# Fresh buffers for the butterflies, later exchange sums, and a down end in five banks, in a fused spectral filter and gated MLP

## The chip, the cores and the metric

The kernel runs on one core of a Trainium2 chip. The metric is the device time of one execution in microseconds (us), the median of several runs. A profile of one execution is read beside it.

## The reference

A layer norm feeds two branches, and their sum is added to the input. One branch is a two-dimensional real FFT over the sequence (2048) and the features (448), a product with a complex filter, and the inverse FFT. The other is a gated MLP with a hidden width of 1792.

```python
def _A_ref(x, w_r, w_i):
    X = jnp.fft.rfft2(x, axes=(-2, -1)) * (w_r + 1j * w_i)
    return jnp.fft.irfft2(X, (S, D), axes=(-2, -1))

def _B_ref(x, W_gate, W_up, W_down):
    gate, up = x @ W_gate, x @ W_up
    return ((gate * (gate > 0)) * up) @ W_down

x = A_x                                   # (1, 2048, 448), f32
xn = _layernorm(x, axis=-1)
return x + _A_ref(xn, A_w_r, A_w_i) + _B_ref(xn, B_W_gate, B_W_up, B_W_down)
```

## The kernel before

**Number format.** Every f32 operand of a matmul is split into a high and a low f16 part, and three matmuls (high by high, high by low, low by high) stand for one. ACT writes the high part, VectorE the low part (value less high part).

**Rows.** The 2048 rows lie as 16 tiles of 128 (`n2` = 0 to 15), in four chunks (`q = n2 % 4`, in the order 0, 2, 1, 3). A tile is normalised (`ln_xn` on VectorE, `ln_hi` on ACT, `ln_lo` on VectorE), and its f16 parts are transposed into `Tq[q]`: in the opening by TensorE or by DMA, in chunks 1 and 3 by DMA (`ln_dma`). `ln_norm` does the first steps for chunks 1 and 3.

**The foreground: the MLP.** The hidden width is 14 blocks of 128 (`f`), in three groups of 5, 5 and 4. A gate unit `("gu", g, f, q)` computes gate and up of one block for one chunk into a PSUM tile of two banks (`gu`, two of them), with 20 full matmuls (L721) and a few of half height (L728). Then `gu_post` runs: relu on ACT (L758), the product with up on VectorE (L762, the last reader of the banks), the high part on ACT (L766) and the low part on VectorE (L770). A down unit `("dn", g, n2)` multiplies all blocks of a group into one PSUM bank (`dn`, two of them; L789), and `dn_post` (L795) adds that to the output tile `xy[:, n2]` on VectorE. After the last gate unit come the four down units of chunk 3: tiles 3, 7, 11 and 15. `store` sends a tile out when both branches have been added.

**The background: the FFT.** It stands in a list `bg` of small steps, each with a cost in us of VectorE. Per tile: a DFT over the features on TensorE (`f_dft`), sums on VectorE (`f_eo`, `f_x`), a split, a DFT over 128 rows (`f_sdft`). Across the 16 tiles: four stages of butterflies on VectorE (`bfly`, called by `f_y1`, `stage2`, `stage3`, `stage4`), on f32 tiles of 128 x 456 in a pool of 17 buffers (`ybuf`, handed out from the list `free`, the last freed first). Then the exchange: `swap` copies the rows 1 to 63 and 65 to 127 crosswise into one of four buffers `sw` by two DMAs on SP's queue (L517, L518), and `pair` adds them (L523, L524). `wmul` multiplies by the filter (L490 to L493). The inverse does the same backwards: butterflies, `i_swap`, `i_pair`, `i_mix` (L590 to L596), splits (L604, L610), `i_sdft` (L620), splits (L625, L628), `i_ddft` (L639) and `i_acc` (L644), which adds to `xy`. `i_sdft` and `i_ddft` use two PSUM banks (`fx`). The list `il` says how many blocks apart the steps of one inverse tile stand.

**The order.** The opening is written out by hand. After that the program walks the units. With each unit it takes background steps from `bg` as long as the unit's credit lasts: a share of the unit's time (`took`) less its own VectorE work (`fixed`). The share is one number, found by bisection so that the background is used up at the unit `last_gu`. Weight preparation is placed by `sched` so many gate units ahead of its use: the down weights' squares, scale, high and low halves (`wd_sq`, `wd_sum`, `wd_scale`, `wd_hi`, `wd_lo`) 4, 3 and 2 units ahead. Within these bounds a list scheduler orders the instructions of each engine; every engine works its own queue in order. All DMAs of this kernel are issued by SP.

Of the kernel before, what the change touches and what calls it, by code (L numbers as in the profile page):

```python
# [42 lines left out]
EXPONE = float(1 << 23)  # L43
NSW = 4
SQ = 2.0 ** -16

# [98 lines left out]
def tile_gfnet_reglu(ctx: ExitStack, tc: tile.TileContext, x, xr, wgu, wd, wf, ident, c_fd, c_fm, c_im, c_row, c_id,  # L145
# [116 lines left out]
    def ln_rstd(q, js=(0, 1, 2, 3), bias=False):  # L262
        w, m = rst[q, js[0]]
        sd, r0, t, r, nm = (w[:, i] for i in range(5))
        V.reciprocal(r0, sd)
        V.scalar_tensor_tensor(t, m[:, :, 1], 1e-5, r0, op0=OP.add, op1=OP.mult)
        V.scalar_tensor_tensor(t, t, -0.5 * 2048, r0, op0=OP.mult, op1=OP.mult)
        V.scalar_tensor_tensor(r, t, 1.5 * 2048, r0, op0=OP.add, op1=OP.mult)
        if bias:
            V.scalar_tensor_tensor(nm, m[:, :, 0], -1.0, r, op0=OP.mult, op1=OP.mult)  # L270
        for i, j in enumerate(js):
            rst[q, j] = r[:, i:i + 1], nm[:, i:i + 1], m[:, i, 0:1]
# [30 lines left out]
    def ln_norm(n2):  # L303
        ln_xn(n2)
        ln_hi(n2)
        ln_copy(n2)
        free.append(xr_b.pop(n2))

    def ln_lo(n2):
        x, t = xn[n2], tt[n2].rearrange("p a b -> p (a b)")  # L310
        V.tensor_tensor(t[:, 512:896], x[:, 0:384], t[:, 0:384], op=OP.subtract)
        twice = [v[:, None, :].to_broadcast([128, 2, 64]) for v in (x[:, 384:448], t[:, 384:448])]
        V.tensor_tensor(tt[n2][:, 3:9:5, 64:128], *twice, op=OP.subtract)
        G.tensor_copy(tt[n2][:, 8, 0:48].rearrange("p (a b) -> p a b", b=16), tt[n2][:, 4:7, 112:128])
        free.append(xn_b.pop(n2))
# [72 lines left out]
    def bfly(a, b, p, sgn):  # L388

        if p == 0:  # L390
            t = free.pop()
            V.tensor_tensor(t, a, b, op=OP.add)  # L392
            V.tensor_tensor(b, a, b, op=OP.subtract)  # L393
            free.append(a)
            return t, b
        t = free.pop()
        if p == 4:
# [17 lines left out]
        V.scalar_tensor_tensor(b, t, f, a, op0=OP.mult, op1=OP.add)  # L415
        V.scalar_tensor_tensor(a, t, -f, a, op0=OP.mult, op1=OP.add)
        free.append(t)
        return b, a

    def f_y1(n2):  # L420
        if n2 < 8:
            t = free.pop()
            A.activation(t, yps[n2], AF.Copy)
            cur["y", n2] = t
        else:
            a, ps = cur.pop(("y", n2 - 8)), yps[n2]
            t = free.pop()
            V.tensor_tensor(t, a, ps, op=OP.add)
            V.tensor_tensor(a, a, ps, op=OP.subtract)
            cur["s1", n2 - 8, 0], cur["s1", n2 - 8, 1] = t, a  # L430

# [53 lines left out]

    def wmul(k2):
        xt, w = cur.pop(("X", k2)), wf_t[k2]
        t = free.pop()
        bc = [w[:, i, :, None, :].to_broadcast([128, 4, 2, KC]) for i in range(2)]
        V.tensor_tensor(t, xt, bc[0], op=OP.mult)  # L490
        V.tensor_tensor(xt, xt, bc[1], op=OP.mult)  # L491
        V.tensor_tensor(t[:, :, 0], t[:, :, 0], xt[:, :, 1], op=OP.subtract)
        V.tensor_tensor(t[:, :, 1], t[:, :, 1], xt[:, :, 0], op=OP.add)  # L493
        free.append(xt)
        cur["V", k2] = t

# [89 lines left out]
    def i_mix(n2):  # L586

        u = cur.pop(("U", n2))
        t = free.pop()
        V.tensor_tensor(t[:, 0:2], u[:, 0:2], u[:, 2:4], op=OP.add)  # L590
        V.tensor_tensor(u[:, 0:2], u[:, 0:2], u[:, 2:4], op=OP.subtract)
        V.tensor_tensor(t[:, 2], t[:, 0], t[:, 1], op=OP.add)
        V.tensor_tensor(t[:, 3], t[:, 0], t[:, 1], op=OP.subtract)
        t2, u2 = (b.rearrange("p g c k -> p (g c) k") for b in (t, u))
        V.tensor_tensor(t2[:, 0:4:3], u2[:, 0:2], u2[:, 3:1:-1], op=OP.subtract)
        V.tensor_tensor(t2[:, 2:0:-1], u2[:, 0:2], u2[:, 3:1:-1], op=OP.add)  # L596
        free.append(u)
        cur["Q", n2] = t
# [194 lines left out]

    def dn_post(g, n2):
        last["V"] = V.scalar_tensor_tensor(xy[:, n2, :], dps[n2][:, 0:D], dsc[:, g:g + 1], xy[:, n2, :],  # L795
                                           op0=OP.mult, op1=OP.add).ins

    def store(n2):

        if n2 in stored:  # L800
            nc.sync.dma_start(ov[:, n2, :], xy[:, n2, :])
        stored.add(n2)

# [9 lines left out]
    def ln_chunk(q):  # L813
        for j in range(4):
            add(0.79, ln_stats, q, j)
        add(0.0, ln_sd, q)
        add(0.7, ln_rstd, q)
        n = [q + 4 * j for j in (0, 2, 1, 3)]
        for t in range(4 + 2):
            for st, (c, fn) in reversed(list(enumerate(((0.51, ln_norm), (0.78, ln_lo), (0.0, ln_dma))))):  # L820
# [5 lines left out]
    fl = ((0.0, f_dft), (0.77, f_eo), (1.08, f_x), (0.63, f_lo), (0.0, f_sdft), (None, f_y1))  # L826
    bf = (1.26, 2.04, 2.04, 2.04, 1.56, 2.04, 2.04, 2.04)

    def fft_chunk(q):
        n = [q + 4 * j for j in (0, 2, 1, 3)]  # L830
        for t in range(4 + len(fl) - 1):
            for st in reversed(range(len(fl))):
                i = t - st
                if 0 <= i < 4:
                    add(fl[st][0] if st < 5 else 1.25 * (n[i] >= 8), fl[st][1], n[i])

# [31 lines left out]
    def back(k0):  # L868
        add(bf[0], inv1, k0)
        if k0 >= 4:  # L870
# [7 lines left out]
            lambda: row_dft(1), row_ev]  # L878
    rows_us = [0.0, 0.8, 0.0, 1.2, 0.0, 0.4, 0.0, 0.8]


    for i0 in range(10):
# [6 lines left out]
        for k in pair_k:  # L889
            add(0.78, pair, ("X", k), 1)  # L890
        if i0 < 8:
            for k in (k0, k0 + 8):
                add(0.0, swap, ("X", k))
        for k in (ks[i0 - 1], ks[i0 - 1] + 8) if 0 < i0 < 9 else ():
            add(0.0, wneg, k)
        for k in pair_k:
            add(2.04, wmul, k)
            add(0.0, wsq, k)
# [4 lines left out]
    add(0.1, wsq_fin)  # L903
    add(0.8, wsq_scale)
    for c, fn in zip(rows_us[4:], rows[4:]):
        add(c, fn)

    def i_wait(n2):
        pass

    il = ((0.0, i_swap), (0.0, i_wait), (0.78, i_pair), (1.86, i_mix), (0.0, i_hi), (0.69, i_lo), (0.0, i_sdft),
          (0.0, i_pqhi), (0.69, i_pqlo), (0.0, i_ddft), (0.68, i_acc))
    io = [n for n0 in range(8) for n in (n0, n0 + 8)]
    for t in range(16 + len(il) - 1):
        if t < 16 and t % 2 == 0:
            add(bf[t // 2], stage4, t // 2, -1, "i3", "U")
        if 3 <= t < 19:
            add(0.0, load_im, io[t - 3])
        for st in reversed(range(len(il))):
# [74 lines left out]
    for g, fs in enumerate(groups):  # L994
        s = max(i for i in gus if i < first["dn", g])
        if g:
            for i, f in enumerate(fs):
                sched(gslot(s, 4), wd_sq, i, f)
            sched(gslot(s, 4), wd_sum, len(fs))
            sched(gslot(s, 3), wd_scale, g, fs)  # L1000
            for i, f in enumerate(fs):
                sched(gslot(s, 2 - i // 2), wd_hi, i, f)
                sched(gslot(s, 2 - i // 2), wd_lo, i, f)
            for i, f in enumerate(fs):
# [75 lines left out]
    took = lambda u: 4.55 if u[0] == "gu" else 0.56 * len(groups[u[1]])  # L1080
    V_US = {"w_scale": 0.33, "w_lo": 0.75, "wd_scale": 1.5, "wd_lo": 0.68}

    def fixed(i):
        c = 1.37 if units[i][0] == "gu" else 0.68
        return c + sum(V_US.get(fn.__name__, 0.0) for fn, a in at.get(i, []))

# [3 lines left out]

    last_gu = max(gus) - 6
    lo, hi = 0.3, 1.2
# [13 lines left out]
    for i, u in list(enumerate(units))[len(groups[0]):]:  # L1106
        is_gu = u[0] == "gu"
        if is_gu:
            _, g, f, q = u
            run_bg(until=marks["T", q])  # L1110
            gu_unit(f, q, (mates.get(u) or (0, 0, None, None))[2:])
        else:
            _, g, n2, _ = u
            dn_mm(groups[g], n2)
        with after(LAG):
# [6 lines left out]
            run_bg(amount=room(i, load[0]) if i >= RAMP else 0.0)  # L1122
        if is_gu:
            with tc.high_priority(offset=400):
# [7 lines left out]
        act_anchors.append(last["A"])  # L1132
    run_bg(until=len(bg))


# [43 lines left out]
```

## Time and profile before

| | before |
|---|---|
| median of three runs | 452.87 us (452.42 to 453.21) |
| profiled execution | 452.37 us, span 450.6 us |
| TensorE (PE) busy | 438.8 us, 97% |
| VectorE (DVE) busy | 390.3 us, 87% |
| ScalarE (ACT) busy | 182.3 us, 40% |
| GpSimd (POOL) busy | 28.1 us, 6% |
| granted TensorE clock | 1.000 |

Busy time is the union of an engine's instructions. Rows of a group read: line, engine, operation, written tile and read tiles, shapes, count, then busy us and mean ns of one, then idle time before them and who ended it. Rows in order of time read: start, length, engine, line, operation, shapes, count of merged instructions, and in brackets the idle time before them and its releaser.

### The profile page before, as it was taken

What the parts mean: (1) busy time and instruction counts of PE and PEld (TensorE: products, weight loads), DVE (VectorE), ACT (ScalarE), POOL (GpSimd) and SP (SyncE); (2) the same over time, 40 slices, a digit from 0 to 9 for tenths busy, and PEclk for the clock granted to TensorE, in tenths of its full rate; (3) what the DMA queues carried; (4) which work ended last, traced back from release to release, by engine and by line L of the source; (5) the groups of instructions that cost most, each with busy time, mean ns of one, the idle gap of its engine ahead of it and who ended that gap; (6) DMA issues with size and microseconds to landing.
All of it is one profiled execution on the core that took longest, in us unless ns stands there. A gap on an engine that the chain in (4) does not pass through costs nothing.

```text
span 450.6 us, 7312 instructions
## 1 busy us (share of the span) xinstructions
PE 438.8 (97%) x2613; PEld 218.2 (48%) x2613; DVE 390.3 (87%) x963; ACT 182.3 (40%) x390; POOL 28.1 (6%) x89
## 2 busy tenths in 40 slices
PE   7999999999999999999999999999999999999996
PEld 3544645455455444444444444444444545655652
DVE  6988799989779888999999999998999997987442
ACT  5887233543545573143134344333234234134120
POOL 2320030200000120000000000000000000000000
PEclk9999999999999999999999999999999999999999
DMA  7939963220002452250320210001111210200202
GB/s 257 328 84 280 397 226 79 49 57 2 1 1 69 154 161 80 84 149 25 90 69 8 83 35 0 1 1 63 62 54 48 90 42 25 88 33 33 89 35 81
DMA packets 39084, 39.61 MB, mean 88 GB/s; under 512 B 18454, under 2 KB 34952, under 8 KB 39048
## 3 DMA queue, kind: packets, MB, share of 16 engines
q1 hardware_dynamic: 39048, 39.15, 27.4%
q8 instruction: 20, 0.33, 0.3%
q14 instruction: 16, 0.13, 0.1%
HBM read 24.38 MB, written 3.67 MB: 62 GB/s over the span
## 4 chain that ended last, share of the span: by engine, by line
PE 48%; DVE 40%; DMA 5%; issue 3%; ACT 2%; SPq 1%; POOL 0%; DVEq 0%; ACTq 0%
PE gu L721 24%; PE dn L789 14%; DVE g L762 4%; DVE h L770 3%; DMA sw<-y 3%; DVE xy L795 2%; PE fx L356 2%; DVE y L490 2%; DVE wt L675 2%; PE fx L386 2%; DVE y L393 2%; PE fx L639 2%; DVE y L392 2%; DVE y L491 2%; PE fx L620 2%
## 5 line engine op out<-in xcount | busy, mean ns | idle before, releaser
L721 PE MATMUL gu<-T,wt 128*128 128x512 f16 (+1 forms) x1140 | 255.9, 375 | 1.6 <-DVE g L762 1.4
L721 PEld LDWEIGHTS <-wt 128*128 128x128 f16 x1140 | 108.8, 98 | 130.1 <-issue 9.7
L789 PE MATMUL dn<-wdt,h 128*128 128x448 f16 x672 | 135.9, 352 | 1.1 <-DVE xy L795 0.9
L789 PEld LDWEIGHTS <-h 128*128 128x128 f16 x672 | 65.1, 98 | 62.8 <-issue 2.6
L766 ACT ACTIVATE h<-g 128x512 f16<-128x512 f32 x56 | 35.0, 626 | 70.7 <-DVE g L762 70.5
L758 ACT ACTIVATE g<-gu 128x512 f32<-128x512 f32 x56 | 33.0, 589 | 72.4 <-PE gu L728 51.5
L770 DVE TENSOR_TENSOR h<-g,h 128x512 f16<-128x512 f32 x56 | 38.3, 686 | 7.2 <-ACT h L766 7.0
L762 DVE SCALAR_TENSOR_TENSOR g<-gu,g 128x512 f32<-128x512 f32 x56 | 38.4, 685 | 6.1 <-ACT g L758 6.0
L795 DVE SCALAR_TENSOR_TENSOR xy<-dn,dsc,xy 128x448 f32<-128x448 f32 x48 | 32.4, 679 | 10.0 <-PE dn L789 10.0
L604 ACT ACTIVATE vt<-y,fsc 128x456 f16<-128x456 f32 x16 | 10.7, 674 | 40.5 <-PE fx L620 26.3
L671 ACT ACTIVATE wt<-wst,wsc 128x512 f16<-128x512 f32 x28 | 19.1, 713 | 5.6 <-DVE wsc L195 5.5
L644 DVE SCALAR_TENSOR_TENSOR xy<-fx,fsc,xy 128x448 f32<-128x448 f32 x16 | 10.8, 681 | 11.6 <-PE fx L639 11.6
L675 DVE SCALAR_TENSOR_TENSOR wt<-wst,wsc,wt 128x512 f16<-128x512 f32 x28 | 20.4, 746 | 0.0
L185 ACT ACTIVATE junk<-wst 128x512 bf16<-128x512 f32 x28 | 17.4, 622 | 2.2 <-DMA wst<-in_wgu 1.9
L728 PE MATMUL gu<-T,wt 64*128 64x512 f16 x112 | 17.0, 381 | 1.1 <-DVE g L762 1.0
L188 POOL PARTITION_ALL_REDUCE wm<-wm x15 | 6.6, 443 | 164.0 <-ACT junk L185 164.0
L523 DVE TENSOR_TENSOR y<-y,sw 128x228 f32<-128x228 f32 x32 | 12.4, 389 | 4.1 <-DMA sw<-y 4.1
L393 DVE TENSOR_TENSOR y<-y,y 128x456 f32<-128x456 f32 x22 | 13.9, 631 | 2.2 <-DMA row<-y 1.7
L377 ACT ACTIVATE Xh<-X 128x456 f16<-128x456 f32 x16 | 9.2, 578 | 14.4 <-PE fx L386 8.1
L625 ACT ACTIVATE pgh<-fx 114x512 f16<-114x512 f32 x16 | 9.5, 592 | 13.1 <-PE fx L639 12.9
L620 PEld LDWEIGHTS <-vt 128*128 128x128 f16 x192 | 12.1, 98 | 4.2 <-issue 0.4
L392 DVE TENSOR_TENSOR y<-y,y 128x456 f32<-128x456 f32 x22 | 13.8, 628 | 0.3
(120 smaller groups left out, 456.7 us busy)
## 6 DMA issues: line engine op xcount, KB each, us to landing
sw<-y SPq DMA_DIRECT2D x64, 112.2 KB
wst<-in_wgu SPq DMA_DIRECT2D x28, 256.0 KB
wf<-in_wf SPq DMA_DIRECT2D x16, 228.0 KB
y<-in_xr SPq DMA_DIRECT2D x16, 224.0 KB
xy<-in_x SPq DMA_DIRECT2D x16, 224.0 KB
out<-xy SPq DMA_DIRECT2D x16, 224.0 KB
wdst<-in_wd SPq DMA_DIRECT2D x14, 224.0 KB
fm<-in_c_fm SPq DMA_DIRECT2D x4, 256.0 KB
```

The lines of the kernel that those rows point to most:

```text
L392: V.tensor_tensor(t, a, b, op=OP.add)
L393: V.tensor_tensor(b, a, b, op=OP.subtract)
L620: P.matmul(o, v[:, h, w], m[:, c, :], start=(i == 0), stop=(i == 2), skip_group_check=True)
L671: A.activation(w[:, 0:4, :], wst[f, g], AF.Copy, scale=wsc[f, g])
L675: V.scalar_tensor_tensor(w[:, 4:8, :], st, sc, w[:, 0:4, :], op0=OP.mult, op1=OP.subtract)
L721: last["P"] = P.matmul(hps[f, q][:, g, cs], wt[f, g][:, a, :], Tq[q][:, b, cs], start=(start and i == 0), stop=(stop and i == len(seq) - 1 ...
L758: last["A"] = A.activation(g1s[f, q], hps[f, q][:, 0, :], AF.Relu, scale=2.0 ** -22).ins
L762: last["V"] = V.scalar_tensor_tensor(g1, hps[f, q][:, 1, :], 2.0 ** -22, g1, op0=OP.mult, op1=OP.mult).ins
L766: A.activation(ht[f, q][:, 0, :], g1s[f, q], AF.Copy)
L770: V.tensor_tensor(h[:, 1, :], g1s.pop((f, q)), h[:, 0, :], op=OP.subtract)
L789: last["P"] = P.matmul(ps[:, 0:D], ht[f, q][:, a, js], wdt[f][:, b, :], start=(i == 0), stop=(i == n - 1)).ins
L795: last["V"] = V.scalar_tensor_tensor(xy[:, n2, :], dps[n2][:, 0:D], dsc[:, g:g + 1], xy[:, n2, :], op0=OP.mult, op1=OP.add).ins
```

## The change

1. A butterfly writes both results into buffers that it takes from the pool, instead of one over an input; `f_y1` and `i_mix` likewise. The pool has 18 buffers, and the one freed longest ago is handed out first.
2. `wmul` does both tiles of a pair with their steps interleaved; `i_mix` has another order of its six operations.
3. In the inverse, `i_pair` and what follows it stand one block later behind `i_swap`.
4. In chunks 1 and 3 ACT subtracts the mean and scales the f16 copy; VectorE's `tensor_scalar` is gone, and the low half multiplies by the row's factor itself.
5. The cost table of the background is new, `last_gu` lies one place later, and the down weights are prepared two gate units earlier.
6. The last four down units become one step, `dn_end`: block by block instead of tile by tile, in five PSUM banks (two `dn`, one half of each `gu` tile, one `fx`), the last tile in two halves of its columns; the additions come behind the last block.

```diff
+LASTGU = 5
-    ybuf = [mt([128, 4, 2, KC], F32, f"y{i}") for i in range(17)]
+    ybuf = [mt([128, 4, 2, KC], F32, f"y{i}") for i in range(18)]
...
+        elif q in CHUNKS[2:]:
+            V.tensor_scalar(nm, m[:, :, 0], -1.0, None, op0=OP.mult)
...
     def ln_norm(n2):
-        ln_xn(n2)
-        ln_hi(n2)
+        xn_b[n2] = free.pop(0)
+        xn[n2] = xn_b[n2].rearrange("p g c k -> p (g c k)")[:, 0:D]
+        r, nm, _ = rst[n2 % 4, n2 // 4]
+        A.activation(xn[n2], xr_t[n2], AF.Identity, bias=nm)
+        new_tt(n2)
+        A.activation(tt[n2].rearrange("p a b -> p (a b)")[:, 0:D], xn[n2], AF.Copy, scale=r)
...
     def ln_lo(n2):
+        if n2 % 4 in CHUNKS[2:]:
+            r = rst[n2 % 4, n2 // 4][0]
+            V.scalar_tensor_tensor(t[:, 512:896], x[:, 0:384], r, t[:, 0:384], op0=OP.mult, op1=OP.subtract)
+            V.scalar_tensor_tensor(tt[n2][:, 3:9:5, 64:128], x2, r, t2, op0=OP.mult, op1=OP.subtract)
...
     def bfly(a, b, p, sgn):
         if p == 0:
-            t = free.pop()
+            t, d = free.pop(0), free.pop(0)
             V.tensor_tensor(t, a, b, op=OP.add)
-            V.tensor_tensor(b, a, b, op=OP.subtract)
-            free.append(a)
-            return t, b
+            V.tensor_tensor(d, a, b, op=OP.subtract)
+            free.extend((a, b))
+            return t, d
...
+        d = free.pop(0)
         V.scalar_tensor_tensor(b, t, f, a, op0=OP.mult, op1=OP.add)
-        V.scalar_tensor_tensor(a, t, -f, a, op0=OP.mult, op1=OP.add)
-        free.append(t)
-        return b, a
+        V.scalar_tensor_tensor(d, t, -f, a, op0=OP.mult, op1=OP.add)
+        free.extend((a, t))
+        return b, d
...
-    def wmul(k2):
+    def wmul(*ks2):
+        ts = []
+        for k2 in ks2:
...
+            V.tensor_tensor(t, xt, bc[0], op=OP.mult)
+            ts.append((t, xt, bc[1]))
+        for t, xt, w in ts:
+            V.tensor_tensor(xt, xt, w, op=OP.mult)
+        for k2, (t, xt, w) in zip(ks2, ts):
+            V.tensor_tensor(t[:, :, 0], t[:, :, 0], xt[:, :, 1], op=OP.subtract)
+            V.tensor_tensor(t[:, :, 1], t[:, :, 1], xt[:, :, 0], op=OP.add)
...
     def i_mix(n2):
+        t, s = free.pop(0), free.pop(0)
+        V.tensor_tensor(s[:, 0:2], u[:, 0:2], u[:, 2:4], op=OP.subtract)
+        V.tensor_tensor(s[:, 2:4], u[:, 0:2], u[:, 2:4], op=OP.add)
+        V.tensor_tensor(t2[:, 0:4:3], s2[:, 0:2], s2[:, 3:1:-1], op=OP.subtract)
+        V.tensor_tensor(t2[:, 2:0:-1], s2[:, 0:2], s2[:, 3:1:-1], op=OP.add)
+        V.tensor_tensor(t[:, 2], s[:, 2], s[:, 3], op=OP.add)
+        V.tensor_tensor(t[:, 3], s[:, 2], s[:, 3], op=OP.subtract)
...
+    def dn_end(g, ns):
+        fs = groups[g]
+        banks = [psum.tile([128, 512], F32, name="dn", bufs=2) for _ in range(2)]
+        banks += [psum.tile([128, 2, 512], F32, name="gu", bufs=2)[:, 0] for _ in range(2)]
+        banks.append(fx())
+        w = [slice(0, D)] * 3 + [slice(0, D // 2), slice(D // 2, D)]
+        parts = list(zip(list(ns) + [ns[-1]], banks, w))
+        for f, n2, ps, cs in ([(f, *p) for f in fs[:-1] for p in parts[:3]] +
+                              [(f, *p) for f in fs[:-1] for p in parts[3:]] + [(fs[-1], *p) for p in parts]):
+            js = slice(128 * (n2 // 4), 128 * (n2 // 4 + 1))
+            for i, (a, b) in enumerate(((0, 0), (0, 1), (1, 0))):
+                P.matmul(ps[:, cs], ht[f, n2 % 4][:, a, js], wdt[f][:, b, cs], start=(f == fs[0] and i == 0),
+                         stop=(f == fs[-1] and i == 2))
+            if f == fs[-1]:
+                dps[n2] = ps
+                with tc.high_priority(offset=400):
+                    dn_post(g, n2, cs)
+                store(n2, cs)
...
-    bf = (1.26, 2.04, 2.04, 2.04, 1.56, 2.04, 2.04, 2.04)
+    bf = (1.09, 1.74, 1.74, 1.74, 1.22, 1.74, 1.74, 1.74)
...
-            add(0.78, pair, ("X", k), 1)
+            add(0.62, pair, ("X", k), 1)
...
+        if pair_k:
+            add(3.4, wmul, *pair_k)
...
-    il = ((0.0, i_swap), (0.0, i_wait), (0.78, i_pair), (1.86, i_mix), (0.0, i_hi), (0.69, i_lo), (0.0, i_sdft),
-          (0.0, i_pqhi), (0.69, i_pqlo), (0.0, i_ddft), (0.68, i_acc))
+    il = ((0.0, i_swap), (0.0, i_wait), (0.0, i_wait), (0.62, i_pair), (1.38, i_mix), (0.0, i_hi), (0.6, i_lo),
+          (0.0, i_sdft), (0.0, i_pqhi), (0.6, i_pqlo), (0.0, i_ddft), (0.6, i_acc))
...
-                sched(gslot(s, 4), wd_sq, i, f)
+                sched(gslot(s, 6), wd_sq, i, f)
...
-    last_gu = max(gus) - 6
+    last_gu = max(gus) - LASTGU
...
-        else:
+        elif i < len(units) - 4:
             dn_mm(groups[g], n2)
...
     run_bg(until=len(bg))
+    dn_end(len(groups) - 1, [u[2] for u in units[-4:]])
```

The cost table changes in every entry in the same way (`V_US`, `fixed` and `rows_us` too); the scale of the down weights moves from 3 to 5 gate units ahead, their halves from 2 to 4.

More of the change, by code (lines that the diff above doesn't have):

```diff
@@ L390, in bfly @@
         if p == 0:
-            t = free.pop()
+            t, d = free.pop(0), free.pop(0)
             V.tensor_tensor(t, a, b, op=OP.add)
-            V.tensor_tensor(b, a, b, op=OP.subtract)
-            free.append(a)
-            return t, b
-        t = free.pop()
+            V.tensor_tensor(d, a, b, op=OP.subtract)
+            free.extend((a, b))
+            return t, d
+        t = free.pop(0)
         if p == 4:
@@ L414, in bfly @@
             V.scalar_tensor_tensor(t[:, :, 1], b[:, :, 1], k, b[:, :, 0], op0=OP.mult, op1=OP.subtract)
+        d = free.pop(0)
         V.scalar_tensor_tensor(b, t, f, a, op0=OP.mult, op1=OP.add)
-        V.scalar_tensor_tensor(a, t, -f, a, op0=OP.mult, op1=OP.add)
-        free.append(t)
-        return b, a
+        V.scalar_tensor_tensor(d, t, -f, a, op0=OP.mult, op1=OP.add)
+        free.extend((a, t))
+        return b, d
     def f_y1(n2):
         if n2 < 8:
-            t = free.pop()
+            t = free.pop(0)
             A.activation(t, yps[n2], AF.Copy)
@@ L426, in f_y1 @@
             a, ps = cur.pop(("y", n2 - 8)), yps[n2]
-            t = free.pop()
+            t, d = free.pop(0), free.pop(0)
             V.tensor_tensor(t, a, ps, op=OP.add)
-            V.tensor_tensor(a, a, ps, op=OP.subtract)
-            cur["s1", n2 - 8, 0], cur["s1", n2 - 8, 1] = t, a
+            V.tensor_tensor(d, a, ps, op=OP.subtract)
+            free.append(a)
+            cur["s1", n2 - 8, 0], cur["s1", n2 - 8, 1] = t, d
     def stage2(j, par, sgn, src, dst):
@@ L484, in wneg @@
         A.activation(w[:, 1, 2:4, :], w[:, 1, 2:4, :], AF.Copy, scale=-1.0)
-    def wmul(k2):
[L487 to L495, printed above, removed]
+    def wmul(*ks2):
+        ts = []
+        for k2 in ks2:
+            xt, w = cur.pop(("X", k2)), wf_t[k2]
+            t = free.pop(0)
+            bc = [w[:, i, :, None, :].to_broadcast([128, 4, 2, KC]) for i in range(2)]
+            V.tensor_tensor(t, xt, bc[0], op=OP.mult)
[5 more added lines that the diff above has]
+            V.tensor_tensor(t[:, :, 1], t[:, :, 1], xt[:, :, 0], op=OP.add)
+            free.append(xt)
+            cur["V", k2] = t
     def inv1(k):
@@ L588, in i_mix @@
         u = cur.pop(("U", n2))
[L589 to L597, printed above, removed]
+        t, s = free.pop(0), free.pop(0)
+        V.tensor_tensor(s[:, 0:2], u[:, 0:2], u[:, 2:4], op=OP.subtract)
+        V.tensor_tensor(s[:, 2:4], u[:, 0:2], u[:, 2:4], op=OP.add)
+        t2, s2 = (b.rearrange("p g c k -> p (g c) k") for b in (t, s))
+        V.tensor_tensor(t2[:, 0:4:3], s2[:, 0:2], s2[:, 3:1:-1], op=OP.subtract)
+        V.tensor_tensor(t2[:, 2:0:-1], s2[:, 0:2], s2[:, 3:1:-1], op=OP.add)
+        V.tensor_tensor(t[:, 2], s[:, 2], s[:, 3], op=OP.add)
+        V.tensor_tensor(t[:, 3], s[:, 2], s[:, 3], op=OP.subtract)
+        free.extend((u, s))
         cur["Q", n2] = t
@@ L792, in dn_mm, with dn_post, store @@
         dps[n2] = ps
-    def dn_post(g, n2):
-        last["V"] = V.scalar_tensor_tensor(xy[:, n2, :], dps[n2][:, 0:D], dsc[:, g:g + 1], xy[:, n2, :],
+    def dn_post(g, n2, cs=slice(0, D)):
+        last["V"] = V.scalar_tensor_tensor(xy[:, n2, cs], dps[n2][:, cs], dsc[:, g:g + 1], xy[:, n2, cs],
                                            op0=OP.mult, op1=OP.add).ins
-    def store(n2):
+    def store(n2, cs=slice(0, D)):
         if n2 in stored:
-            nc.sync.dma_start(ov[:, n2, :], xy[:, n2, :])
-        stored.add(n2)
+            nc.sync.dma_start(ov[:, n2, cs], xy[:, n2, cs])
+        if cs.stop == D:
+            stored.add(n2)
+    def dn_end(g, ns):
[16 more added lines that the diff above has]
+                store(n2, cs)
     bg = []
@@ L814, in ln_chunk @@
         for j in range(4):
-            add(0.79, ln_stats, q, j)
+            add(0.63, ln_stats, q, j)
         add(0.0, ln_sd, q)
-        add(0.7, ln_rstd, q)
+        add(0.6, ln_rstd, q)
         n = [q + 4 * j for j in (0, 2, 1, 3)]
         for t in range(4 + 2):
-            for st, (c, fn) in reversed(list(enumerate(((0.51, ln_norm), (0.78, ln_lo), (0.0, ln_dma))))):
+            for st, (c, fn) in reversed(list(enumerate(((0.0, ln_norm), (0.68, ln_lo), (0.0, ln_dma))))):
                 i = t - st
@@ L1080, in tile_gfnet_reglu @@
     took = lambda u: 4.55 if u[0] == "gu" else 0.56 * len(groups[u[1]])
-    V_US = {"w_scale": 0.33, "w_lo": 0.75, "wd_scale": 1.5, "wd_lo": 0.68}
+    V_US = {"w_scale": 0.2, "w_lo": 0.66, "wd_scale": 1.1, "wd_lo": 0.6}
     def fixed(i):
-        c = 1.37 if units[i][0] == "gu" else 0.68
+        c = 1.2 if units[i][0] == "gu" else 0.6
         return c + sum(V_US.get(fn.__name__, 0.0) for fn, a in at.get(i, []))
@@ L1122, in tile_gfnet_reglu @@
             run_bg(amount=room(i, load[0]) if i >= RAMP else 0.0)
+        if i >= len(units) - 4:
+            continue
         if is_gu:
```

28 lines of the change are left out of this document (14 added, 14 removed).

## The prediction

> **What bounds the kernel now.** I read the page's first two parts, then the busy time by stretch, then the waits of TensorE, then the order of time around its longest wait and around the end.
>
> ```profile
> span 450.6 us, 7312 instructions
> PE 438.8 (97%) x2613; PEld 218.2 (48%) x2613; DVE 390.3 (87%) x963; ACT 182.3 (40%) x390; POOL 28.1 (6%) x89
> ```
>
> TensorE is busy for 438.8 of 450.6 us, and the change takes no matmul away: 11.8 us is all there is to win. The stretches show where it lies (columns: stretch, length, then PE, PEld, DVE, ACT, POOL busy).
>
> ```profile
> 45.00:110.00 65.00, 65.00 (x416) 33.44 (x415) 59.01 (x161) 23.94 (x54) 7.52 (x25) 1.00 0.45 141
> 180.00:314.00 134.00, 133.79 (x661) 60.94 (x660) 128.22 (x289) 46.81 (x109) 3.53 (x6) 1.00 0.17 51
> 314.00:354.00 40.00, 36.64 (x232) 18.81 (x230) 39.67 (x112) 13.73 (x24) 0.00 (x0) 1.00 0.18 54
> 354.00:437.00 83.00, 83.00 (x642) 46.75 (x641) 62.47 (x143) 25.03 (x41) 0.00 (x0) 1.00 0.17 56
> ```
>
> In 314 to 354 TensorE stands for 40.00 - 36.64 = 3.36 us, while VectorE is busy for 39.67 of 40. In 180 to 314 it stands for 0.21 with VectorE at 128.22 of 134 (96%); in 354 to 437, with VectorE at 75%, never. The rest is the end, and the opening, whose written-out order the diff leaves alone. The waits of TensorE from 180 us on name the culprits (us, times, longest):
>
> ```profile
> PE gu L721 <- DVE g L762: 1.4, 1, 1.4
> PE gu L728 <- DVE g L762: 1.0, 1, 1.0
> PE dn L789 <- DVE xy L795: 0.9, 2, 0.6
> ```
>
> These are PSUM banks that VectorE emptied late. VectorE's own waits from 300 to 316, and the order of time, show what held it up before the longest:
>
> ```profile
> DVE y L523 <- DMA sw<-y: 2.0, 2, 1.2
> ```
> ```profile
> 315.44 0.69 DVE L762 SCALAR_TENSOR_TENSOR g<-gu,g 128x512 f32<-128x512 f32 x1
> ...
> 316.18 4.04 PE L721 MATMUL gu<-T,wt 128*128 128x512 f16 x18 [1.37 <-DVE g L762]
> ```
>
> VectorE waited 2.0 us for exchanges (`swap`) that had not landed; the gated product (L762) stood behind those sums on its in-order queue, and 1.37 us of TensorE behind the product.
>
> **The change part by part.**
>
> *Fresh buffers, and products in another order.* Here the spacing of starts is the price, not the duration.
>
> ```profile
> 252.87 0.63 DVE L392 TENSOR_TENSOR y<-y,y 128x456 f32<-128x456 f32 x1
> 253.53 0.63 DVE L393 TENSOR_TENSOR y<-y,y 128x456 f32<-128x456 f32 x1
> ```
> ```profile
> 325.89 0.62 DVE L415 SCALAR_TENSOR_TENSOR y<-y,y 128x456 f32<-128x456 f32 x1
> 326.44 0.68 DVE L762 SCALAR_TENSOR_TENSOR g<-gu,g 128x512 f32<-128x512 f32 x1
> ```
> ```profile
> 330.03 0.39 DVE L523 TENSOR_TENSOR y<-y,sw 128x228 f32<-128x228 f32 x1
> 330.34 0.39 DVE L524 TENSOR_TENSOR y<-y,sw 128x228 f32<-128x228 f32 x1
> ```
> ```profile
> 402.08 0.39 DVE L590 TENSOR_TENSOR y<-y 128x228 f32<-128x228 f32 x1
> ...
> 403.00 0.69 DVE L762 SCALAR_TENSOR_TENSOR g<-gu,g 128x512 f32<-128x512 f32 x1
> 403.61 0.27 DVE L593 TENSOR_TENSOR y<-y 128x114 f32<-128x114 f32 x1
> 403.91 0.28 DVE L595 TENSOR_TENSOR y<-y 128x114 f32<-128x114 f32 x1
> 404.10 0.27 DVE L596 TENSOR_TENSOR y<-y 128x114 f32<-128x114 f32 x1
> ```
>
> L393 writes over what L392 reads and starts 0.66 us after it. L762 has nothing to do with L415 and starts 0.55 us after it, before L415 has ended. So a dependent neighbour costs 0.11 us more. There are 22 + 20 + 8 such pairs by the code (L392/393, L415/416, L428/429): 50 x 0.11 = 5.5 us, but nothing where another instruction already stands between the two, as L762 does behind L415. `wmul` has two such steps in each of 16 calls: 16 x 0.22 = 3.5 us. `i_mix` takes 404.10 + 0.19 - 402.08 - 0.61 (the slot of L762) = 1.60 us, and at the independent spacing (0.31 as from L523 to L524, 0.19 as from L595 to L596) 2 x 0.31 + 4 x 0.19 = 1.38: 16 x 0.22 = 3.5 us. Bounds of the three together: 0 and 12.5 us of VectorE; I take 9, nearer the upper end because the row of the plain butterfly shows the neighbours together.
>
> [...]
>
> *Rows centred by ACT.* In chunks 1 and 3 eight instructions leave VectorE; ACT gets eight more, and its f16 copy a scale.
>
> ```profile
> 82.73 1.78 DVE L287 TENSOR_SCALAR y<-y,mv,rs 128x448 f32<-128x448 f32 x4
> ```
> ```profile
> L296 ACT ACTIVATE tt<-y 128x448 f16<-128x448 f32 x12 | 6.2, 567 | 0.6 <-DVE y L287 0.5
> ...
> L294 ACT ACTIVATE tt<-y,rs 128x448 f16<-128x448 f32 x4 | 3.0, 749 | 1.0 <-DVE rs L270 1.0
> ```
>
> VectorE loses 8 x 0.44 = 3.5 us (four in 1.78); ACT gains between 8 x 0.567 and 8 x (0.749 + 0.182), 4.5 to 7.4 us. The new instructions wait for the row factors from VectorE, and the foreground's relu can queue behind them; POOL's copies, VectorE's low halves and SP's transposes wait for them in turn. All this lies in 45 to 110, where ACT is busy for 23.94 of 65.00 us and TensorE never stands: nothing on the path. Without that cover it would be the 0.6 to 0.9 us that one row takes longer, once per chunk.
>
> *Down weights two gate units earlier.* Per group this moves four or five squares (ACT), an all-reduce (POOL), VectorE's short scale chain, and the high (ACT) and low (VectorE) halves; it moves no DMA. In 314 to 354 these rows stand:
>
> ```profile
> L707 DVE SCALAR_TENSOR_TENSOR wdt<-wdst,wds,wdt 128x448 f16<-128x448 f32 x4 | 2.5, 676 | 0.0
> L590 DVE TENSOR_TENSOR y<-y 128x228 f32<-128x228 f32 x6 | 2.3, 391 | 0.1
> ```
>
> Four low halves (2.5 us) leave, and six mixes shrink (6 x 0.22 = 1.3): 3.8 us of VectorE, more than TensorE stood. The halves fall on earlier units, whose background the planner cuts by their cost.
>
> *Exchange sums one block later.* Same instructions; the 2.0 us ahead of L762 go. Late next is the mix, and nothing of the foreground waits for that. One of four exchange buffers comes free a block later, so SP may hold a swap, with the stores and `im` loads behind it.
>
> *Background spread anew.* By the old cost table the background adds up to 282.5 us, and the planner needs a share of 1.08 of each unit's time; by the new one it is 228.5 us and 0.89 (the kernel's own arithmetic: shares, no times). It hands out work closer to VectorE's real spacing, and ends one gate unit later.
>
> For these parts together the stake is the 3.36 + 0.21 = 3.57 us of standing. Bounds: all of it goes; or none does, and more comes. VectorE would have (39.67 - 3.8) of the remaining 36.6 us, 98%; the nearest row, 180 to 314, stands 0.21 us at 96%. I take **-3.0 us**.
>
> *The down end.*
>
> ```profile
> 442.24 4.70 PE L789 MATMUL dn<-wdt,h 128*128 128x448 f16 x24 [0.59 <-DVE xy L795]
> ```
> ```profile
> 441.51 1.28 DVE L795 SCALAR_TENSOR_TENSOR xy<-dn,dsc,xy 128x448 f32<-128x448 f32 x2 [1.64 <-PE dn L789]
> 444.71 0.68 DVE L795 SCALAR_TENSOR_TENSOR xy<-dn,dsc,xy 128x448 f32<-128x448 f32 x1 [1.93 <-PE dn L789]
> 446.98 0.68 DVE L795 SCALAR_TENSOR_TENSOR xy<-dn,dsc,xy 128x448 f32<-128x448 f32 x1 [1.59 <-PE dn L789]
> ```
>
> Two banks hold two tiles, and the third tile waits 0.59 us for a bank. With five banks that goes. Matmuls come every 0.19 us (24 in 4.70); twelve become 24 of half the width, estimated at 0 to 0.1 us more. But all additions now come behind the last weights. Counted from the last matmul, three whole ones 0.60 apart (two take 1.28) and two halves about 0.31 apart end after 0.82 us instead of 0.72; and the four tiles' stores follow within 2 us instead of being spread over six. From the end of the last addition (447.66) to the end of the span (450.6) pass 2.9 us, which half a store keeps nearly whole; behind the other stores it may lose 0.1 to 0.9 us. I take -0.59 + 0.05 + 0.10 + 0.10 = **-0.35 us**, bounds -0.9 and +0.5.
>
> [...]
>
> **Sum.** The profiled execution took 452.37 us, 1.8 more than its span; less 3.35 that is 449.0. The median of the three runs, 452.87, lies 0.5 above it; on that scale the prediction is **449.5 us**, and the best case 452.87 - 3.57 - 0.9 = 448.4.
>
> **Rivals.**
>
> *Order frees nothing.* The new neighbours stay 0.66 apart, or the freed slots fill with work that the planner moved forward; the 3.57 us of standing turn up at another place, and only the end gains: 452.87 - 0.35 = 452.5, no change. For it: VectorE is at 96 to 99% from 180 to 354, and 18 buffers for 16 values leave two spare ones, so that a fresh one is often one just read. Against: the spacings of 0.55 and 0.31. [...]
>
> *The background outlasts the down end* (slower). The last column transforms trail at a set pace:
>
> ```profile
> 422.56 0.83 PE L620 MATMUL fx<-im,vt 128*128 128x128 f16 x12
> ...
> 428.46 0.83 PE L620 MATMUL fx<-im,vt 128*128 128x128 f16 x12
> ...
> 434.47 1.35 PE L639 MATMUL fx<-idc_t,pgh 114*128 114x112 f16 x24
> ```
>
> One comes every 5.9 us, the last ends at 435.8, and the fifth bank of the end is one of theirs. Ended 10.4 us later, by one gate unit (estimated at 4.5 us, 20 full passes and the halves) and one step of that pace, it would be at 446.2. The accumulation that frees the bank (0.68), twelve half matmuls (1.2), the half addition (0.39) and the store (2.9) then end at 451.4, which is 453.7 on the scale of the median. From there on every us counts whole; half a step more (2.9) gives 456.6. Against it: the plan puts the last exchange sum into the same unit as before.
>
> **How the numbers follow.** Forecast, most of the standing gone (448.4 to 451.2): 0.66. Order frees nothing (452 to 453.7): 0.18. Background past the end, or a new wait of its size: 0.16. A difference of 0.2% (0.9 us) is about what a measurement of this kernel can tell from none; so faster 0.66, same 0.18, slower 0.16. The range leaves out the slower cases and a little below the best: 448.2 to 453.3. The forecast's own is 448.2 to 451.2.
>
> **What would show it.** Right: TensorE full from 180 to the end but for about half a microsecond; no wait of L523 for `sw` ahead of L762; the second instruction of a butterfly 0.55 behind the first; VectorE's busy time lower, and TensorE's unchanged; five additions at the end, the last ending near 0.8 us after the last matmul. Wrong: waits of `gu` or `dn` matmuls for VectorE at other places; the last inverse transform behind 442; more than 3.5 us from the last matmul to the end of the last store.

## The result and the profile after

The changed kernel takes 447.77 us (median; 447.27 to 448.09), the kernel before 452.76 beside it: ratio 0.9888, 95% interval 0.9871 to 0.9905. It is faster by 5.0 us; forecast were 3.35, and 447.77 lies 0.4 us below the range. The profiled execution took 448.09 us.

The first parts of its page:

```profile
span 446.3 us, 7350 instructions
PE 437.7 (98%) x2625; PEld 219.1 (49%) x2625; DVE 381.9 (86%) x958; ACT 188.2 (42%) x398; POOL 34.3 (8%) x89
```

The same stretches as before (stretch, length, then PE, PEld, DVE, ACT, POOL busy), and the waits of TensorE from 22 us to the end:

```profile
45.00:110.00 65.00, 65.00 (x416) 33.51 (x415) 57.19 (x162) 27.76 (x57) 8.46 (x25) 1.00 0.51 145
...
180.00:314.00 134.00, 134.00 (x664) 61.08 (x662) 128.77 (x300) 49.39 (x113) 8.59 (x6) 1.00 0.17 53
314.00:354.00 40.00, 40.00 (x253) 20.75 (x251) 35.79 (x98) 11.32 (x19) 0.00 (x0) 1.00 0.17 54
354.00:437.00 83.00, 83.00 (x643) 46.79 (x641) 60.92 (x137) 25.36 (x42) 0.00 (x0) 1.00 0.15 50
```
```profile
PE gu L740 <- DVE wt L694: 0.2, 1, 0.2
```

From 45 us on TensorE never stands; the one wait left is in the opening. A good mark between opening and rest is the first down matmul, which stands at the same place in both programs (order of time on TensorE, before and after):

```profile
42.84 0.54 PE L789 MATMUL dn<-wdt,h 128*128 128x448 f16 x2
```
```profile
43.74 0.54 PE L808 MATMUL dn<-wdt,h 128*128 128x448 f16 x2
```

The end of the changed kernel, in order of time (VectorE and TensorE; the last matmul ends at 442.07 + 0.45 = 442.52):

```profile
442.05 1.03 DVE L814 SCALAR_TENSOR_TENSOR xy<-gu,dsc,xy 128x448 f32<-128x448 f32 x2
442.07 0.45 PE L836 MATMUL fx<-wdt,h 128*128 128x224 f16 x3
443.00 0.44 DVE L814 SCALAR_TENSOR_TENSOR xy<-fx,dsc,xy 128x224 f32<-128x224 f32 x1
```

So the 4.3 us between the two spans are these: the opening of this execution is 0.90 us longer (43.74 against 42.84; the spans of the four executions, 445.5 to 446.3, differ by nearly as much). The change did not lengthen it: in the five experiments below that start from the kernel before, the mark stands at 43.29 to 43.73. From the mark to the end of the last matmul it is 398.78 against 404.10 us, 5.32 less. From there to the end of the span it is 3.78 against 3.66, 0.12 more. Of the 5.32, 4.16 are idle time that the profile of before recorded (3.57 in the middle, 0.59 in the end). The other 1.16 stood in no idle time.

Where it stood can be read from one group's row, of the changed kernel:

```profile
L740 PE MATMUL gu<-T,wt 128*128 128x512 f16 (+1 forms) x1140 | 255.6, 375 | 0.2 <-DVE wt L694 0.2
```

One matmul is shown for 375 ns, but a run of 20 without a wait takes 4.48 us (the one at 98.06 us, for instance), so the next starts (4.48 - 0.375) / 19 = 0.216 us after it. A wait begins where the shown end is; 0.375 - 0.216 = 0.16 us of standing before that are shown as busy. Six recorded waits hide about 1 us in this way; measured were 1.16.

On VectorE the spacing of a butterfly's last pair is what was forecast, 0.54 us in place of 0.66:

```profile
244.59 0.62 DVE L404 TENSOR_TENSOR y<-y,y 128x456 f32<-128x456 f32 x1
245.13 0.62 DVE L405 TENSOR_TENSOR y<-y,y 128x456 f32<-128x456 f32 x1
```

### The profile page after: what moved, and what is told of

Its sections match the earlier page's. It is cut to its first block, busy times and chain, and to the rows that moved or that the text cites. A ratio compares the mean times of both kernels' runs of the same rounds, so it can differ in the third digit from the quotient of the medians.

```text
span 446.3 us, 7350 instructions
## 1 busy us (share of the span) xinstructions
PE 437.7 (98%) x2625; PEld 219.1 (49%) x2625; DVE 381.9 (86%) x958; ACT 188.2 (42%) x398; POOL 34.3 (8%) x89
## 4 chain that ended last, share of the span: by engine, by line
PE 91%; DMA 3%; DVE 3%; issue 1%; SPq 0%; ACT 0%; POOL 0%; DVEq 0%; ACTq 0%
PE gu L740 51%; PE dn L808 26%; PE gu L747 3%; PE fx L639 2%; PE fx L368 2%; PE fx L658 2%; DMA wst<-in_wgu 2%; PE fx L398 2%; DMA y<-in_xr 1%; PE dn L836 1%; DVE wt L694 1%; PE gu L836 1%; DVE g L781 0%; DVE y L290 0%; DVE xy L814 0%
## 5 line engine op out<-in xcount | busy, mean ns | idle before, releaser
L808 PE MATMUL dn<-wdt,h 128*128 128x448 f16 x624 | 127.0, 352 | 0.0
L808 PEld LDWEIGHTS <-h 128*128 128x128 f16 x624 | 60.3, 98 | 56.4 <-issue 0.4
L814 DVE SCALAR_TENSOR_TENSOR xy<-dn,dsc,xy 128x448 f32<-128x448 f32 x46 | 31.0, 676 | 12.3 <-PE dn L808 7.8
L189 POOL PARTITION_ALL_REDUCE wm<-wm x15 | 11.7, 779 | 167.8 <-ACT junk L186 167.8
L250 DVE BATCH_NORM_STATS2 bst<-y 128x6 f32<-128x448 f32 x16 | 9.7, 612 | 4.9 <-DMA y<-in_xr 4.9
L639 PE MATMUL fx<-im,vt 128*128 128x128 f16 x192 | 13.5, 219 | 0.0
```

The source lines that it names most:

```text
L639: P.matmul(o, v[:, h, w], m[:, c, :], start=(i == 0), stop=(i == 2), skip_group_check=True)
L808: last["P"] = P.matmul(ps[:, 0:D], ht[f, q][:, a, js], wdt[f][:, b, :], start=(i == 0), stop=(i == n - 1)).ins
L814: last["V"] = V.scalar_tensor_tensor(xy[:, n2, cs], dps[n2][:, cs], dsc[:, g:g + 1], xy[:, n2, cs], op0=OP.mult, op1=OP.add).ins
```

## The experiments

Each kernel is the changed one with a part undone, or the kernel before with a part done. The work from the first down matmul to the end of the last matmul is the length to compare, as the opening varies; it is 398.8 us where nothing stands.

**The old steps in the changed kernel.**

```diff
     def bfly(a, b, p, sgn):
         if p == 0:
-            t, d = free.pop(0), free.pop(0)
+            t = free.pop()
             V.tensor_tensor(t, a, b, op=OP.add)
-            V.tensor_tensor(d, a, b, op=OP.subtract)
+            V.tensor_tensor(b, a, b, op=OP.subtract)
...
-            add(3.4, wmul, *pair_k)
+            [add(1.7, wmul, k) for k in pair_k]
```

> The changed kernel with the old butterflies, f_y1, i_mix and wmul (in place, last freed first); pool of 18, plan, exchange distance, normalisation and down end stay as changed. Theory 1 (VectorE had fallen behind, and the cheaper neighbours are what lets it keep up): 50 pairs, wmul and i_mix cost about 9 us of VectorE again, waits of matmuls for VectorE come back after 180 us, 1.5 to 4 us slower than 447.8, so 449.3 to 451.8. Theory 2 (the new spread of the background does it, the freed VectorE time lies off the path): no wait of TensorE comes back, 447.8 to 448.3.

447.52 us (447.42 to 448.05), no slower than the changed kernel. Its page and its stretch from 314 to 354:

```profile
PE 438.6 (98%) x2625; PEld 219.0 (49%) x2625; DVE 388.0 (87%) x958; ACT 187.8 (42%) x398; POOL 32.9 (7%) x89
```
```profile
314.00:354.00 40.00, 40.00 (x252) 20.71 (x251) 36.33 (x96) 12.30 (x22) 0.00 (x0) 1.00 0.19 60
```

VectorE works 6.1 us longer (388.0 against 381.9), and TensorE does not notice: the work is 398.87 us. Theory 2: with the new plan, the fresh buffers are off the path.

**The old plan in the changed kernel.** The whole old cost table, `last_gu`, and the down weights' places:

```diff
-    bf = (1.09, 1.74, 1.74, 1.74, 1.22, 1.74, 1.74, 1.74)
+    bf = (1.26, 2.04, 2.04, 2.04, 1.56, 2.04, 2.04, 2.04)
...
-                sched(gslot(s, 6), wd_sq, i, f)
+                sched(gslot(s, 4), wd_sq, i, f)
...
-LASTGU = 5
+LASTGU = 6
```

> The changed kernel with the old cost table, the old last_gu and the down weights prepared 4, 3 and 2 gate units ahead; all code of the steps stays as changed. Theory 1 (cheaper neighbours): at most 0.7 us slower than 447.8. Theory 2 (the spread): TensorE stands again near the down weights of the last group, 2 to 4 us slower, 449.8 to 451.8.

449.21 us (448.93 to 449.62), 1.4 slower; the work is 399.84 us, 1.06 more. Two waits came back:

```profile
PE gu L747 <- DVE g L781: 0.9, 2, 0.7
```

That is between the two theories' numbers: with the cheap steps in place the plan is worth little, but not nothing.

**The old down end in the changed kernel.**

```diff
-    dn_end(len(groups) - 1, [u[2] for u in units[-4:]])
...
-        elif i < len(units) - 4:
+        else:
             dn_mm(groups[g], n2)
```

> The changed kernel with the old down end (tile by tile, two banks). The wait of 0.59 us for a bank comes back; if a recorded wait costs TensorE some 0.16 us more than its own length (the matmul before it is counted as busy past the next start), and the additions of the old end finish 0.1 to 0.2 us earlier behind the last matmul, the sum is 0.6 us slower than 447.8: 448.4. If the end is worth nothing: 447.8; if it is worth more than its wait: 449 and above.

448.48 us (447.92 to 448.55), 0.7 slower. Its work is 399.51 us, 0.73 more, for one wait of 0.59:

```profile
438.42 4.70 PE L808 MATMUL dn<-wdt,h 128*128 128x448 f16 x24 [0.59 <-DVE xy L814]
```

For a single wait the hidden part is thus 0.14 us. Two kernels below, the one before with the new table and with the whole new plan, have the same single wait and give 0.14 and 0.35, so one such reading is good to about 0.2 us. The tail from the last matmul to the end of the span is 3.68 us, 0.10 shorter than with the new end.

**Another order for the new end.** The changed end finishes all five parts on the last block of weights; this one finishes the three whole tiles first.

```diff
-        for f, n2, ps, cs in ([(f, *p) for f in fs[:-1] for p in parts[:3]] +
-                              [(f, *p) for f in fs[:-1] for p in parts[3:]] + [(fs[-1], *p) for p in parts]):
+        for f, n2, ps, cs in ([(f, *p) for f in fs for p in parts[:3]] + [(f, *p) for p in parts[3:] for f in fs]):
```

> The changed kernel with another order of the down end: the three whole tiles are finished, block by block, before the last tile's two halves are begun. Theory A (the last addition starts 0.5 us behind the last matmul because five additions queue on VectorE): the last addition starts within 0.1 us of it, 0.4 us faster, 447.4. Theory B (the stores' own time sets the end, whatever the additions do): no change. Theory C (the fourth and fifth bank come free too late, or the last block's low part): a wait of TensorE in the end, slower.

447.02 us (446.56 to 447.22; ratio to the kernel before 0.9869, 0.9853 to 0.9886): below every run of the changed kernel, 0.75 us by the medians. Its last matmuls and its last addition:

```profile
440.85 1.31 PE L835 MATMUL fx<-wdt,h 128*128 128x224 f16 x12
```
```profile
442.20 0.45 DVE L814 SCALAR_TENSOR_TENSOR xy<-fx,dsc,xy 128x224 f32<-128x224 f32 x1 [0.70 <-PE fx L835]
```

The addition starts 0.04 us behind the last matmul (442.16), not 0.48, and the work is the same 398.79 us. From the end of the last addition to the end of the span it is about 2.6 us, and was 2.9: the stores queue less too. In the changed kernel the packets of the five stores run in one block without a gap, and the last packet ends 1.6 us behind the last addition; here the last store starts after a gap of 0.7 us, and its last packet ends 1.3 us behind the last addition. Theory A, and some more.

**The old exchange distance in the changed kernel.**

```diff
-    il = ((0.0, i_swap), (0.0, i_wait), (0.0, i_wait), (0.62, i_pair),
+    il = ((0.0, i_swap), (0.0, i_wait), (0.62, i_pair),
```

> The changed kernel with the exchange sums of the inverse at their old distance from the swap. Theory X (the exchange that had not landed is the cause of the longest wait): VectorE waits 1 to 2 us for sw ahead of a gated product, and TensorE stands for 1 to 2 us, with 0.16 us more for each wait: 449 to 450. Theory S (VectorE now has slack enough to wait for it): VectorE's waits for sw come back, TensorE's do not, 447.6 to 448.1.

447.80 us (447.67 to 447.82), no change; the work is 398.79 us. Theory S for the changed kernel: the distance is not needed there. But VectorE's waits did not come back either, as both theories had it. Its one wait for `sw`, 0.54 us at 181 us, belongs to the forward exchange and stands in the changed kernel too (0.27); in the inverse it waits once, 0.53 us, for the exchange's row (`row`, row 64 of the tile, which `i_swap` brings by a DMA of its own).

**The exchange distance alone, in the kernel before** (the same edit the other way; in both, the loads of `im` move by a block with it).

> The kernel before with the exchange sums of the inverse one block later, and nothing else. Theory X: the wait of 1.37 us for L762 near 316 goes, the others stay, 1.2 to 1.8 us faster than 452.8, so 451 to 451.6. Theory P: the late product is a matter of how much stands on VectorE there, the waits move, 452.3 to 453.2.

453.17 us, ratio 1.0014 (0.9999 to 1.0028): no gain. The waits of TensorE from 45 us on, and VectorE's exchange sums ahead of the product near 316:

```profile
PE gu L721 <- DVE g L762: 3.2, 2, 2.6
PE dn L789 <- DVE xy L795: 1.2, 2, 0.6
```
```profile
311.31 0.40 DVE L523 TENSOR_TENSOR y<-y,sw 128x228 f32<-128x228 f32 x1 [0.65 <-DMA sw<-y]
...
313.57 0.40 DVE L523 TENSOR_TENSOR y<-y,sw 128x228 f32<-128x228 f32 x1 [0.95 <-DMA sw<-y]
```

The edit hardly takes away what it was meant to: the two waits are 0.65 and 0.95 us, and were 0.72 and 1.23. TensorE's stop near 316 shrank to 0.62 us, and the one near 336 grew from 1.04 to 2.59. Theory P, by its number: the waits move.

**Old steps and old plan in the changed kernel.** The first two edits together.

> The changed kernel with both the old in-place steps and the old plan (cost table, last_gu, places of the down weights); exchange distance, normalisation and down end stay as changed. Theory S (the cheaper steps and the plan stand in for each other: either alone keeps VectorE ahead): much more than the 1.4 us that the old plan alone cost, 450.3 to 452.3. Theory P (the plan alone counts, the cheaper steps lie off the path): as with the old plan alone, 448.9 to 449.7.

455.78 us (454.33 to 455.96): 8.0 us slower than the changed kernel, 2.8 slower than the kernel before (453.00 beside it), and more than either theory said. Undone alone, the steps cost nothing and the plan 1.4 us. They stand in for each other: either one keeps TensorE nearly full, and without both it falls behind. The waits of TensorE from 45 us on, and the longest in order of time:

```profile
PE gu L733 <- DVE g L774: 5.3, 3, 2.8
PE dn L801 <- DVE xy L807: 0.4, 1, 0.4
```
```profile
337.61 6.16 PE L733 MATMUL gu<-T,wt 128*128 128x512 f16 x20 [2.81 <-DVE g L774]
```

The work is 406.81 us, 8.0 more. The idle time explains 5.7 of that. The 20 matmuls behind the longest stop took 6.16 us in place of 4.48, another 1.7; more on that in the last section. The other 0.7 us are what the four stops hide. Two of the five executions took only 454.33 and 454.64 us, which is still 1.3 to 1.6 more than the kernel before: the exchange distance, the rows centred by ACT and the new end, without the cheaper steps and the new plan, lose. Which of them brings the stop of 1.85 us near 193 was not separated.

**The plan alone, in the kernel before.**

```diff
-    bf = (1.26, 2.04, 2.04, 2.04, 1.56, 2.04, 2.04, 2.04)
+    bf = (1.09, 1.74, 1.74, 1.74, 1.22, 1.74, 1.74, 1.74)
...
-                sched(gslot(s, 4), wd_sq, i, f)
+                sched(gslot(s, 6), wd_sq, i, f)
...
-    last_gu = max(gus) - 6
+    last_gu = max(gus) - 5
```

> The kernel before with the new cost table, last_gu one later and the down weights prepared two gate units earlier; steps in place, exchange distance, normalisation and down end as before. Theory P or S: the standing of 3.6 us from 180 to 354 goes, and 0.16 us for each of its waits, 4.4 us in all, 448.5 to 449.5. If the exchange distance is needed too (Theory X): the wait behind L523 stays, 449.8 to 451.

448.41 us (ratio 0.9899, 0.9884 to 0.9914): nearly the whole gain, without one cheaper instruction; the work is 399.72 us. Of TensorE's recorded waits only the end's 0.59 is left. Theory X falls: the plan does it at the old exchange distance.

**The fresh buffers alone, in the kernel before.** The steps of the first experiment the other way, with the pool of 18; old costs.

> The kernel before with the fresh buffers alone: butterflies, f_y1, wmul and i_mix as changed, a pool of 18 handed out in order; old plan, old exchange distance, old normalisation, old down end. Theory S (the cheaper steps and the plan stand in for each other): as the changed kernel with the old plan (449.2) and the old end (0.7 us more), 449.5 to 450.5. Theory P (only the plan counts): no change, 452.4 to 453.4.

449.61 us (ratio 0.9927, 0.9912 to 0.9942), as theory S had it: 3.2 us, with one stop left in the middle and that of the end. The stop in the middle, and a wait of VectorE for the exchange's row ahead of the product that it hung on (307.94):

```profile
304.12 0.40 DVE L530 TENSOR_TENSOR y<-y,sw 128x228 f32<-128x228 f32 x1 [2.72 <-DMA y<-row]
```
```profile
308.67 0.61 PE L735 MATMUL gu<-T,wt 64*128 64x512 f16 x4 [1.01 <-DVE g L769]
```

**The plan in two halves.** First the cost table and `last_gu` alone, the down weights at their old places.

> The kernel before with the new cost table and the later last_gu alone; the down weights are prepared 4, 3 and 2 gate units ahead as before. With table and places both new it took 448.4. If the table (how much background each unit gets) does it: 448.2 to 449.2. If the places of the down weights do it: the standing near 340 stays, 450.5 to 452.5.

448.42 us (ratio 0.9900, 0.9885 to 0.9915), the same as the whole plan. The work is 399.50 us, 4.60 less than in the kernel before. Its stretches:

```profile
45.00:180.00 135.00, 135.00 (x813) 67.47 (x812) 119.49 (x315) 61.64 (x141) 19.28 (x43) 1.00 0.36 113
180.00:314.00 134.00, 134.00 (x664) 61.20 (x663) 129.54 (x294) 48.42 (x112) 3.91 (x6) 1.00 0.16 49
314.00:354.00 40.00, 40.00 (x253) 20.65 (x251) 39.01 (x107) 13.43 (x23) 0.00 (x0) 1.00 0.16 51
```

VectorE is at 39.01 of 40 us from 314 to 354, nearly as full as in the kernel before (39.67), and TensorE stands not once. So the share of VectorE was not what the stops hung on. Its work stands otherwise: 1.32 us more is done between 180 and 314 (129.54 against 128.22), and even a wait of 1.82 us for the exchange's row, in the order of time on VectorE, stops no matmul:

```profile
307.76 0.40 DVE L523 TENSOR_TENSOR y<-y,sw 128x228 f32<-128x228 f32 x1 [1.82 <-DMA y<-row]
```

Whether the table does this or the later `last_gu` was not separated.

Then the places of the down weights alone:

```diff
-                sched(gslot(s, 4), wd_sq, i, f)
+                sched(gslot(s, 6), wd_sq, i, f)
...
-            sched(gslot(s, 3), wd_scale, g, fs)
+            sched(gslot(s, 5), wd_scale, g, fs)
```

> The kernel before with the down weights prepared two gate units earlier (6, 5 and 4) and nothing else; old cost table. If the places do it: TensorE no longer stands near 340 and 353, 449 to 450.5. If the table does it: the crowd on VectorE moves to other units and TensorE stands there, 452 to 454.

451.48 us (ratio 0.9974, 0.9962 to 0.9985), 1.3 faster, between the two theories' numbers. The stop of 1.37 us near 316 and the one of 0.21 near 191 are gone, the one near 340 shrank to 0.16 us, and another near 352 grew from 0.48 to 1.57:

```profile
336.71 0.61 PE L728 MATMUL gu<-T,wt 64*128 64x512 f16 x4 [0.16 <-DVE g L762]
349.33 0.83 PE L620 MATMUL fx<-im,vt 128*128 128x128 f16 x12 [0.23 <-DVE pgh L628]
351.73 0.76 PE L639 MATMUL fx<-idc_t,pgh 114*128 114x112 f16 x12 [1.57 <-DVE xy L644]
```

**A narrower last addition**, on top of the staggered end.

```diff
-        w = [slice(0, D)] * 3 + [slice(0, D // 2), slice(D // 2, D)]
+        w = [slice(0, D)] * 3 + [slice(0, 336), slice(336, D)]
```

> The changed kernel with the staggered down end (447.0) and its last tile cut at column 336 instead of 224. The last addition has 112 columns, about 0.27 us as L592's 114 in place of 0.45: if the length of the last addition counts, 0.1 to 0.2 us faster, 446.9, which lies within the interval of a comparison; if the stores' short rows (448 bytes) cost more than that, 447.0 or slower. The profile's distance from the last matmul to the end of the span tells it: 2.9 us before this step.

446.90 us (446.61 to 447.33; ratio 0.9865, 0.9848 to 0.9881): not to be told from the 447.02 of the staggered end. The narrow addition is short, but queues behind the wide one:

```profile
442.04 0.57 DVE L814 SCALAR_TENSOR_TENSOR xy<-gu,dsc,xy 128x336 f32<-128x336 f32 x1 [0.98 <-PE gu L835]
442.63 0.33 DVE L814 SCALAR_TENSOR_TENSOR xy<-fx,dsc,xy 128x112 f32<-128x112 f32 x1
```

From its last matmul to the end of the span it is 3.00 us, against 3.04 (the expectation's 2.9 was a little short).

## Why the prediction was wrong

*Where it failed: the term of 3.0 us for the standing in the middle, which measured 4.6, in two ways.* It counted recorded idle time as all that there was to win ("11.8 us is all there is"), and took TensorE's busy time as fixed. From the mark to the last matmul that fell from 399.94 (404.10 - 4.16) to 398.78 us, with twelve matmuls more, because each wait hides 0.1 to 0.2 us in the matmul before it; even the bound of 3.57 us was too low. And it left 0.57 us of the 3.57 standing, by the row of a stretch where VectorE was equally full. That stretch's 0.21 us was no wait for VectorE but for ACT, which prepared the down weights late:

```profile
191.04 0.54 PE L789 MATMUL dn<-wdt,h 128*128 128x448 f16 x2 [0.21 <-ACT wdt L703]
```

With the new table alone VectorE is busy for 129.54 of the same 134 us, and TensorE never stands there. The middle gave 5.32 - 0.73 = 4.6 us, and 4.60 by the table alone.

*The end* was mis-sized the same way: 0.35 us forecast, 0.7 measured by the old end in the changed kernel. The wait for a bank was worth 0.73 in place of 0.59, and the tail grew by 0.12 in place of 0.20. Together 1.6 + 0.3 us are what the forecast of 3.35 missed of the 5.0, within the scatter of the openings. The packets of SP's last store took 0.46 us for the half store of the staggered end and 0.76 for the whole one of the kernel before, 0.30 less.

*The cause was shared out wrongly,* though the sum did not depend on it. The fresh buffers' saving is real: 0.54 us between neighbours, 6.1 us of VectorE (9 was taken, of a bound of 12.5). It was taken too high in part because only 25 of the 50 pairs stood next to each other in the kernel before, worth 25 x 0.12 = 3.0 us and not 5.5. Alone it brings 3.2 us, and beside the new table nothing. The table with the later `last_gu` brings 4.4 us alone, and the down end's 0.7 on top make up the whole 5.0. The later exchange sums, which were to remove the origin of the longest stop, earn nothing with the old plan and nothing with the new: alone they shortened the waits ahead of it only from 1.95 to 1.60 us. Whether those waits caused that stop was therefore not shown. With the fresh buffers alone, a wait of 2.72 us for the row stands ahead of the stop of 1.01; with the new table, one of 1.82 us caused none, and the places of the down weights alone removed the longest stop at the old distance.

*What held.* TensorE is full from 45 us to its end, the five additions end 0.92 us behind the last matmul (0.82 forecast), and ACT's extra work, 5.9 us (4.5 to 7.4), costs nothing. The centring alone was not run, and that it is worth nothing beside the new table is by difference only; VectorE's fall beyond the 6.1 us of the fresh buffers is 2.3 us, where 3.5 were taken.

*The rivals.* "Order frees nothing" failed on its spacing, and its event, standing that turns up at another place, is what the exchange distance and the down weights' places brought when tried alone. "The background outlasts the down end" did not come: the last inverse transform starts at 434.34 us, and started at 434.47.

## What to carry to other kernels

Where an engine is full but for a few stops, price a stop by the length from one fixed instruction to another in two kernels, not by its recorded idle time, which here left out 0.1 to 0.2 us of each wait. Freeing time on the next busiest engine and placing its work better can be two ways to the same gain: undo each alone before crediting either, and both together to see what they guard against. At the end of a kernel, finish what can be finished early, so that one short addition and one short store stand behind the last matmul (0.75 us here, by the medians of the changed kernel and the staggered end).

## What the hardware showed unexpectedly

In the kernel with old steps and old plan TensorE stopped for 2.81 us, and its granted clock (the column behind POOL) was halved for some 3.4 us after it (by that column 1.26 of the first 1.40 us, the next 2.00, and 0.16 of the 2.00 behind them):

```profile
334.00:337.60 3.60, 0.80 (x4) 0.28 (x3) 3.60 (x14) 0.01 (x1) 0.00 (x0) 1.00 0.26 79
337.60:339.00 1.40, 1.39 (x4) 0.55 (x4) 1.40 (x5) 1.11 (x2) 0.00 (x0) 0.55 0.31 99
339.00:341.00 2.00, 2.00 (x6) 0.72 (x5) 2.00 (x7) 0.71 (x2) 0.00 (x0) 0.50 0.34 107
341.00:343.00 2.00, 2.00 (x11) 0.85 (x10) 2.00 (x6) 2.00 (x4) 0.00 (x0) 0.96 0.02 8
```

That cost 6.16 - 4.48 = 1.7 us beyond the stop.

In the profiles the clock stayed at 1.00 behind stops of 2.59 us (the exchange distance alone) and 1.85 us (old steps and old plan, near 193). But the length of the stop may not decide alone, by the times and mean clocks of the other executions. Of the five with old steps and old plan, three took 455.78 to 455.96 us at a mean clock of 0.992 to 0.996, and two 454.33 and 454.64 at 1.000; 3.4 us at half speed, 1.7 of the 454.1 us of that profile's span, would make 0.996. With the exchange distance alone, three of ten took 454.80 to 455.04 us at 0.995 to 0.996, and seven 452.69 to 453.27 at 0.998 to 1.000. With the down weights' places alone, one of ten took 453.73 us at 0.996, and nine 451.23 to 451.93 at 0.999 to 1.000. A low mean by itself proves little, since one execution of the kernel before had 0.996 at 452.96 us. There is one profile of each kernel, so which stop slowed the clock in those executions, and what decides it, stays open.
